# A feed-forward's first product from seven block products in groups of 768 tokens

## The chip, the cores and the metric

The kernel runs on one core of a Trainium2 chip, which has a matmul engine (PE, with its weight loads shown apart as PEld), VectorE (DVE), ScalarE (ACT), GpSimd (POOL) and SyncE (SP); SP issues nearly all DMAs here. The metric is the device time of one execution in microseconds, the median of several runs. Before the change it was 1222.69 us (three runs, 1220.99 to 1223.44).

## The reference

Three layers follow one another. An attention between 512 tokens and 32 state rows, in 8 batches and 8 heads, gives 4608 rows of 512 numbers. A mixture of 8 experts sends each row with a positive score to one expert. The last layer, which is changed here, is a feed-forward over all 4608 rows:

```python
def _moe2_ref(x, w_in, w_out):        # x 4608 x 512, w_in 512 x 2048, w_out 2048 x 512
    h = x @ w_in
    relu6 = np.clip(h + 3.0, 0.0, 6.0)
    g = h * relu6 / 6.0
    return (g @ w_out).astype(np.float32)
```

## The kernel before

Everything is float32. In this layer PE multiplies in the type `float32r`, so each operand is split: `hi` is the value cast to `float32r` (by ACT), `lo` the remainder (by DVE or POOL), and a product is the sum of three matmuls, hi by hi, hi by lo and lo by hi (`PAIRS`). 4608 tokens are 36 chunks of 128; `w_in` and `w_out` are cut into 16 blocks f of 128 hidden columns (`NFF`).

The feed-forward takes the chunks in groups of four (512 tokens), and one group of two. For a group j and a block f, `stage_a` (L1269) multiplies w_in's block by the group's transposed tokens: 12 matmuls of 512 columns (256 in the small group), three for each quarter of the 512 inputs, all into one PSUM bank. Then the gate: Relu with a bias on ACT, minimum and multiplication on DVE, the cast on ACT, the remainder on DVE. Two steps later `stage_b` (L1289) multiplies the gate by w_out's block, three matmuls of 512 columns for each chunk, adding up over all f in a PSUM bank of its own per chunk. Only after the last f is the sum scaled by 1/6 and written out. The tokens are transposed on PE and split (`turn`, L1245).

The split weights of all 16 blocks lie in SBUF for the whole stage (`W1` for w_in, `W2` for w_out). The inputs of weights are first turned from 64-bit numbers into float32 by four DVE steps a block (`Weights.cut`). That happens beside the earlier layers; blocks 0 to 2 are split right there and kept in SBUF (`steps`, L1176), blocks 3 to 15 are stored to DRAM as float32 (`keep`, L1182, tensor `w32`) and read again in the feed-forward (`again`, L1187), where `convert` splits them while the first group runs.

There is no scheduler: engines run their instructions in the order in which the code names them (`manual_schedule`), and wait on semaphores where a tile is not ready or its buffer is not free. A tile pool with `bufs=3` gives a tag three buffers; a fourth tile of that tag waits until all that used the first, DMAs among them, is done. SP too works in order: a DMA whose data is not ready keeps all later ones of SP from being issued. The tensors of the first two layers, the loops over experts (`item_a`, `item_b`) and their DMAs stay as they are.

Of the kernel before, what the change touches and what calls it, by code (L numbers as in the profile page):

```python
# [9 lines left out]
F32 = mybir.dt.float32  # L10
# [10 lines left out]
P = 128  # L21
# [656 lines left out]
class Experts:  # L678
# [108 lines left out]
    def run(self, ctx, c2, tail, plan, after):  # L787
# [272 lines left out]
        scatter_a()  # L1060
        turned32(xb[:, 0:DM], x32)
# [34 lines left out]
NPRE = 3  # L1096
# [9 lines left out]
class Weights:  # L1106


    def __init__(self, tc, ctx, w_in, w_out):
        self.tc, self.w_in, self.w_out = tc, w_in, w_out  # L1110
        self.rp = ctx.enter_context(tc.tile_pool(name="w_r", bufs=2))
        self.W1, self.W2, self.raw = {}, {}, {}
        self.w32 = tc.nc.dram_tensor("w32", (NFF, 2, P, DM), F32, kind="Internal").ap()
        self.alloc(ctx.enter_context(tc.tile_pool(name="w_c", bufs=1)), range(NPRE))

    def alloc(self, pool, fs):
        for f in fs:
            self.W1[f] = [pool.tile([P, 4, P], F32R, name=f"W1_{i}_{f}") for i in range(2)]
            self.W2[f] = [pool.tile([P, DM], F32R, name=f"W2_{i}_{f}") for i in range(2)]
# [61 lines left out]

# [5 lines left out]
    def again(self, f):  # L1187

        t = self.raw[f] = [self.room(i) for i in range(2)]
        for i in range(2):  # L1190
            self.tc.nc.sync.dma_start(t[i], self.w32[f, i])  # L1191


def ffn(tc, ctx, W, x_in, out, k):

# [48 lines left out]

    def turn(c0):  # L1245

        j, c = divmod(c0, 4) if c0 < 32 else (B, c0 - 32)
        if c == 0:
            new_xt(j)
        if j in (0, B):  # L1250

            pt = p_o.tile([P, 4, P], F32, tag=f"o{c + j // 2}", name="ptx")
        else:
            pt = p_h.tile([P, 4, P], F32, tag="h", name="ptx")
        for kk in range(4):
            nc.tensor.transpose(pt[:, kk, :], xw[c0][:, P * kk:P * kk + P], ident)  # L1256
        hi, lo = ([a[:, :, P * c:P * c + P] for a in t] for t in (xt[j] if j == 1 else [[a] for a in whole[j]]))
        parts = pt.rearrange("p (i k) t -> i p k t", i=len(hi))
        for i, h in enumerate(hi):
            nc.scalar.copy(h, parts[i])  # L1260

        def low():
            for i, h in enumerate(hi):
                nc.vector.tensor_tensor(lo[i], parts[i], h.bitcast(F32), op=ALU.subtract)  # L1264
        return low
# [3 lines left out]
    def stage_a(j, f):  # L1269
        n = P * len(cols(j))  # L1270
        ph = p_h.tile([P, 512], F32, tag="h", name="ph")
        i = 0
        for kk in range(4):
            for a, b in PAIRS:
                nc.tensor.matmul(  # L1275
                    ph[:, :n], lhsT=W1[f][a][:, kk, :], rhs=xt[j][b][kk // 2][:, kk % 2, :n],
                    start=(i == 0), stop=(i == 11),
                )
                i += 1
        gg = sp.tile([P, 512], F32, tag="gg", name="gg", bufs=1)  # L1280
        nc.scalar.activation(gg[:, :n], ph[:, :n], AF.Relu, bias=k["three"])  # L1281
        nc.vector.scalar_tensor_tensor(gg[:, :n], gg[:, :n], 6.0, ph[:, :n], op0=ALU.min, op1=ALU.mult)  # L1282
        hi, lo = g[j, f] = [sp.tile([P, 512], F32R, tag=f"g{i}", name=f"g{i}", bufs=3) for i in range(2)]
        nc.scalar.copy(hi[:, :n], gg[:, :n])  # L1284
        nc.vector.tensor_tensor(lo[:, :n], gg[:, :n], hi[:, :n].bitcast(F32), op=ALU.subtract)  # L1285

    po, o = {}, {}

    def stage_b(j, f):  # L1289
        gg = g.pop((j, f))  # L1290
        for c, c0 in enumerate(cols(j)):
            if f == 0:
                po[c0] = p_o.tile([P, DM], F32, tag=f"o{c + (4 if j == B else 0)}", name=f"po{c}")
            for i, (a, b) in enumerate(PAIRS):
                nc.tensor.matmul(  # L1295
                    po[c0], lhsT=gg[a][:, P * c:P * c + P], rhs=W2[f][b],
                    start=(f == 0 and i == 0), stop=(f == NFF - 1 and i == 2),
                )
            if f == NFF - 1:
                if j in (0, B):  # L1300
                    oc = W.room(c % 2)
                else:
                    if c % 2 == 0:
                        o[c // 2] = W.scratch(c // 2).bitcast(F32).rearrange("p (c f) -> p c f", c=2)
                    oc = o[c // 2][:, c % 2, :]
                if c % 2:
                    nc.scalar.mul(oc, po[c0], 1.0 / 6.0)  # L1307
                else:
                    nc.vector.tensor_scalar(oc, po[c0], 1.0 / 6.0, None, op0=ALU.mult)
                if 0 < j < B - 1 or (j == B - 1 and c < 2):  # L1310
                    if c % 2:
                        for p, rows in rows_of(out, c0 - 1):
                            nc.sync.dma_start(rows, o[c // 2][p])
                else:
                    for p, rows in rows_of(out, c0 - c % 2):
                        nc.sync.dma_start(rows[:, c % 2], oc[p])

    later = [0, 2, 32] + list(range(4, 32, 2))

    def fetch_after(c0):  # L1320

        n = later.index(c0 - 1) + 2 if c0 % 2 else len(later)
        if n < len(later):
            fetch(later[n])

    conv = []
    for f in range(NPRE, NFF):
        conv += [(f, lambda f=f, i=i: W.split(f, i, W.raw[f][i], nc.vector)) for i in range(2)]
        if f + 2 < NFF:
            conv.append((f, lambda f=f: W.again(f + 2)))  # L1330

    def convert(n, until=-1):

        while conv and (n > 0 or conv[0][0] <= until):
            conv.pop(0)[1]()
            n -= 1

    W.again(NPRE)
    W.again(NPRE + 1)
    fetch(0)  # L1340
    fetch(2)
    low = None
    for c in range(4):
        if low:
            low()
        low = turn(c)
        fetch_after(c)
    low()


    work = [(0, 0), (0, 1)]
    for f in range(2, NFF + 2):
        work += [(0, f)] * (f < NFF) + [(B, f - 2)]
    both = len(work)
    work += [(j, f) for j in range(1, B) for f in range(NFF)]

    turns = {1: [32, 33]}
    for c in range(4):
        turns[both - 5 + c] = [4 + c]
        for j in range(2, B):  # L1360
            turns[both + (j - 2) * NFF + 3 * c + 2] = [4 * j + c]
    last = both - 6
    total = len(conv)
    LAG = 2
    for n in range(len(work) + LAG):
        if n < len(work):
            f = work[n][1]
            if n < both:
                convert(len(conv) - total * max(0, last - n) // last, f + 1)
            stage_a(*work[n])  # L1370
        if n >= LAG:
            stage_b(*work[n - LAG])
        for low in [turn(c0) for c0 in turns.get(n, ())]:
            low()
        for c0 in turns.get(n, ()):
            fetch_after(c0)
# [132 lines left out]
```

## Time and profile before

| what | value |
|---|---|
| median of three runs | 1222.69 us |
| the profiled execution, its own time | 1233.33 us |
| its span, first to last instruction | 1231.6 us |
| mean granted PE clock | 0.984 of full |
| PE busy over the span | 1176.7 us (96%), 5916 matmuls |
| DVE, ACT, POOL busy | 537.9, 439.0, 118.8 us |
| feed-forward, first transpose to last matmul | 466.1 to 1226.6 us |
| moved by DMA over the span | 132.05 MB |

The profile is one execution taken by the hardware profiler. It took 10.6 us more than the median of the runs, so times inside it are read as they stand, and a difference between two kernels is compared with the runs. Matmuls are pipelined: a single row's duration is longer than the distance between two of them, and the distance is what counts.

### The profile page before, as it was taken

How to read it: one execution, taken by the hardware profiler on the slowest of the kernel's cores; microseconds unless marked ns; L12 is line 12 of the kernel's file. 1: busy time of each engine (PE TensorE's matmuls, PEld its weight loads, DVE VectorE, ACT ScalarE, POOL GpSimd, SP SyncE). 2: the span in 40 equal slices, each digit the busy share in tenths (PEclk: the TensorE clock that was granted, in tenths of full speed). 3: DMA queues.
4: the chain of work that ended last, by engine and by line, in shares of the span. 5: the costliest groups of instructions: out<-in, count | busy, mean ns of one | idle time of the engine just before them, and what ended most of it. 6: DMA issues, size and time to landing. Idle time of an engine off the chain costs nothing.

```text
span 1231.6 us, 16493 instructions
## 1 busy us (share of the span) xinstructions
PE 1176.7 (96%) x5916; PEld 945.1 (77%) x5916; DVE 537.9 (44%) x984; ACT 439.0 (36%) x802; POOL 118.8 (10%) x162
## 2 busy tenths in 40 slices
PE   7988898999998968999999999999999999999998
PEld 4565767887886647888888888888888888888886
DVE  6968596876873004443422322322232322322222
ACT  7865353443543103333422222322222222322222
POOL 4556131011011000000000000000000000000000
PEclk9989899999999988999999999999999999999999
DMA  7956667587585784220200000000000000000000
GB/s 194 312 193 213 213 229 248 173 280 253 169 283 180 264 289 131 69 61 27 76 27 18 35 18 18 35 18 18 35 18 18 35 18 18 35 1 1 35 1 34
DMA packets 83535, 132.05 MB, mean 107 GB/s; under 512 B 12176, under 2 KB 49040, under 8 KB 82704
## 3 DMA queue, kind: packets, MB, share of 16 engines
q1 hardware_dynamic: 78832, 119.63, 29.8%
q0 software_dynamic: 4640, 11.57, 2.6%
q8 instruction: 40, 0.66, 0.2%
q14 instruction: 23, 0.19, 0.0%
HBM read 91.55 MB, written 43.30 MB: 109 GB/s over the span
## 4 chain that ended last, share of the span: by engine, by line
PE 62%; DMA 0%; SPq 0%; DVE 0%; ACT 0%; issue 0%
PE ph L1275 30%; PE po L1295 30%; PE ptx L1256 1%; DMA xw<-x_in_dram 0%; SPq L1191 0%; DVE xt L1264 0%; ACT raw L1307 0%; ACT xt L1260 0%; SPq L1229 0%
## 5 line engine op out<-in xcount | busy, mean ns | idle before, releaser
L1295 PE MATMUL po<-W,g 128*128 128x512 f32 x1632 | 393.5, 389 | 0.0
L1295 PEld LDWEIGHTS po<-W,g 128*128 128x128 f32 x1632 | 305.3, 188 | 62.7
L1275 PE MATMUL ph<-xt,W 128*128 128x512 f32 (+1 forms) x1536 | 351.5, 378 | 1.0 <-ACT xt L1260 0.7
L1275 PEld LDWEIGHTS ph<-xt,W 128*128 128x128 f32 x1536 | 275.5, 188 | 54.0 <-ACT xt L1260 0.9
L1282 DVE SCALAR_TENSOR_TENSOR gg<-gg,ph 128x512 f32<-128x512 f32 (+1 forms) x144 | 94.9, 659 | 388.6 <-ACT gg L1281 388.6
L1281 ACT ACTIVATE gg<-ph,three 128x512 f32<-128x512 f32 (+1 forms) x144 | 95.9, 666 | 394.7 <-PE ph L1275 394.6
L1285 DVE TENSOR_TENSOR g<-gg,g 128x512 fp32r<-128x512 f32 (+1 forms) x144 | 95.5, 663 | 97.5 <-ACT g L1284 95.1
L860 PE MATMUL ph<-xTa,w1p 128*128 128x512 f32 x480 | 121.0, 403 | 4.5 <-DVE w1p L775 1.8
L1284 ACT CAST g<-gg 128x512 fp32r<-128x512 f32 (+1 forms) x144 | 86.1, 598 | 104.6 <-DVE gg L1282 104.6
L872 PE MATMUL po<-w2p,hT 128*128 128x512 f32 x480 | 120.9, 398 | 0.4 <-ACT hT L864 0.3
L860 PEld LDWEIGHTS ph<-xTa,w1p 128*128 128x128 f32 x480 | 92.3, 193 | 27.3 <-DVE w1p L775 2.5
L872 PEld LDWEIGHTS po<-w2p,hT 128*128 128x128 f32 x480 | 89.0, 188 | 21.4 <-DVE hT L865 0.8
L1275 PE MATMUL ph<-raw,W 128*128 128x512 f32 x192 | 46.6, 391 | 0.0
L277 PE MATMUL pxr<-BD,AT 128*128 128x265 f32 x128 | 41.3, 442 | 3.8 <-ACT XR L281 1.9
L1275 PEld LDWEIGHTS ph<-raw,W 128*128 128x128 f32 x192 | 35.7, 188 | 7.3
L775 DVE TENSOR_TENSOR w1p<-raw,w1p 128x512 fp32r<-128x512 f32 x48 | 32.0, 685 | 20.3 <-ACT w1p L774 10.2
L1160 ACT ACTIVATE raw<-raw 128x512 f32<-128x512 f32 x32 | 22.0, 686 | 47.9 <-DVE cv L1156 47.8
L864 ACT ACTIVATE hT<-ph 128x512 fp32r<-128x512 f32 x40 | 23.9, 596 | 42.5 <-PE ph L860 38.9
L1264 DVE TENSOR_TENSOR xt<-ptx,xt 128x512 fp32r<-128x512 f32 x30 | 20.6, 691 | 38.7 <-ACT xt L1260 38.6
L378 POOL DMA_INDIRECT xs_dram<-XR,slot x32 | 32.9, 1028 | 39.8 <-issue 20.2
L774 ACT CAST w1p<-raw 128x512 fp32r<-128x512 f32 x48 | 28.5, 618 | 20.3 <-DMA raw<-in_moe_w_dram 20.3
L865 DVE SCALAR_TENSOR_TENSOR hT<-ph,hT 128x512 fp32r<-128x512 f32 x40 | 27.5, 687 | 18.7 <-ACT hT L864 16.0
(218 smaller groups left out, 932.9 us busy)
## 6 DMA issues: line engine op xcount, KB each, us to landing
raw<-in_moe_w_dram SPq DMA_DIRECT2D x80, 512.0 KB, 6.3
raw<-in_moe_w_in_dram SPq DMA_DIRECT2D x16, 512.0 KB
raw<-in_moe_w_out_dram SPq DMA_DIRECT2D x16, 512.0 KB, 8.2
x_in_dram<-XR SPq DMA_DIRECT2D x8, 1024.0 KB
xw<-x_in_dram SPq DMA_DIRECT2D x14, 512.0 KB
w<-cv SPq DMA_DIRECT2D x26, 256.0 KB, 3.1
cv<-w SPq DMA_DIRECT2D x26, 256.0 KB
out_dram<-raw SPq DMA_DIRECT2D x13, 512.0 KB
```

What stands on the lines that cost most here:

```text
L277: nc.tensor.matmul(px, lhsT=AT[b, q][:, P * c:P * c + P], rhs=BD[:, 2 * b + q, :], start=True, stop=True,)
L378: i = nc.gpsimd.indirect_dma_start(out=xs, out_offset=bass.IndirectOffsetOnAxis(ap=slot[:, col:col + 1], axis=0), in_=t["rows"][c], in_off ...
L774: nc.scalar.copy(hi, src)
L775: (eng or nc.vector).tensor_tensor(lo, src, hi.bitcast(F32), op=ALU.subtract)
L860: nc.tensor.matmul(ph, lhsT=w1p[a][:, f, kk, :], rhs=xTa[b][:, kk, :], start=(n == 0), stop=(n == 11))
L872: nc.tensor.matmul(po[c], lhsT=hp[f][a][:, P * c:P * c + P], rhs=w2p[b][:, f, :], start=(f == 0 and n == 0), stop=(f == NF - 1 and n == 2),)
L1275: nc.tensor.matmul(ph[:, :n], lhsT=W1[f][a][:, kk, :], rhs=xt[j][b][kk // 2][:, kk % 2, :n], start=(i == 0), stop=(i == 11),)
L1281: nc.scalar.activation(gg[:, :n], ph[:, :n], AF.Relu, bias=k["three"])
L1282: nc.vector.scalar_tensor_tensor(gg[:, :n], gg[:, :n], 6.0, ph[:, :n], op0=ALU.min, op1=ALU.mult)
L1284: nc.scalar.copy(hi[:, :n], gg[:, :n])
L1285: nc.vector.tensor_tensor(lo[:, :n], gg[:, :n], hi[:, :n].bitcast(F32), op=ALU.subtract)
L1295: nc.tensor.matmul(po[c0], lhsT=gg[a][:, P * c:P * c + P], rhs=W2[f][b], start=(f == 0 and i == 0), stop=(f == NFF - 1 and i == 2),)
```

## The change

The first product is computed for pairs of blocks of f, p = 0 to 7, and for groups of six chunks (768 tokens). The weights of a pair and the tokens of a group are each taken as 2 x 2 blocks: w_in by halves of the 512 inputs and by the pair's two f, the tokens by halves of the inputs and into two halves of 384 tokens. Seven products of such blocks (in place of eight), with sums and differences of blocks as operands, give all four blocks of the result after seven additions on DVE (`strassen`). Each product is 6 matmuls of 384 columns. The second product of a pair follows one pair later: 36 matmuls of 512 columns, in six PSUM groups that are added to a sum in SBUF by DVE (by ACT for p = 0).

The combinations of the weights are made once. The first four chunks (the two of state rows and the first two) go through all 16 f in the old way. During this first round the weights come from `w32`, are split, combined (`combine`) and stored to two DRAM tensors, `wc` and `wo`; the split weights no longer stay in SBUF but have three buffers per matrix. Afterwards 40 pairs (five groups of eight) load 1.84 MB of `wc` and 1.05 MB of `wo` each. The tokens' combinations are made in `turn`. Blocks 0 to 2 are now kept in `w32` as the others are, and the first two are read again before the loop of the small experts.

```diff
         scatter_a()
+        for f in range(2):
+            for i in range(2):
+                self.W.again(f, i)
         turned32(xb[:, 0:DM], x32)
...
+    groups = [list(range(c, c + 6)) for c in range(2, 32, 6)]
...
+    def new_w(i, f):
+        (W1, W2)[i][f] = t = sp.tile([P, 2, DM], F32R, tag=f"W{i}", name=f"W{i}", bufs=3)
+        return t
+
+    def split_w(i, f):
+        t = new_w(i, f)
+        split(t[:, 0], t[:, 1], W.raw[f, i])
+
+    def combine(p):
...
+        v.tensor_tensor(s[0], a2[0], a2[1], op=ALU.add)
+        v.tensor_tensor(s[2], a1[0], a2[0], op=ALU.subtract)
+        v.tensor_tensor(s[1], s[0], a1[0], op=ALU.subtract)
+        v.tensor_tensor(s[3], a1[1], s[1], op=ALU.subtract)
+        both = qp.tile([P, 2, 2 * DM], F32R, tag="both", name="both", bufs=2)
+        split(both[:, 0], both[:, 1], t)
+        nc.sync.dma_start(W.wc[p, :, 3 * DM:].rearrange("p (i f) -> p i f", i=2), both.bitcast(F32))
+
+    def store_w(f):
+        p, o = divmod(f, 2)
+        if o == 0:
+            nc.sync.dma_start(W.wc[p, :, 0:2 * DM], W1[f].bitcast(F32).rearrange("p i f -> p (i f)"))
         else:
+            nc.sync.dma_start(
+                W.wc[p, :, 2 * DM:3 * DM].rearrange("p (i f) -> p i f", i=2), W1[f][:, :, 2 * P:].bitcast(F32)
+            )
...
+    for f in range(NFF + LAG):
+        if f < NFF:
+            stage_a(f)
+            if f + 2 < NFF:
+                load_w(0, f + 4)
+                split_w(0, f + 2)
+                if f % 2:
+                    combine((f + 2) // 2)
+            if f + 1 < NFF:
+                split_w(1, f + 1)
+                load_w(1, f + 3)
+        if f >= LAG:
+            stage_b(f - LAG)
+        if f < NFF:
+            store_w(f)
+            store_o(f)
...
+        if f >= NFF - 2:
+            load_c(f - NFF + 2) if f < NFF else load_o(f - NFF)
...
+        p1 = product(m, A11, B11)
+        nc.scalar.copy(c1, p1)
+        plus(u2, product(m, S2, T2), c1)
+        plus(u5, product(m, S1, T1), u2)
+        p7 = product(m, S3, T3)
+        plus(c22, p7, u5)
+        plus(u2, p7, u2)
+        plus(c1, product(m, A12, B21), c1)
+        done(1, 1, c22)
+        plus(u5, product(m, S4, B22), u5)
+        done(0, 0, c1)
+        plus(u2, product(m, A22, T4), u2)
+        return [lambda: done(0, 1, u5), lambda: done(1, 0, u2)]
...
+        between = []
+        if m < total:
+            between = strassen(m)
+            load_c(m + 2)
+        if m > 0:
+            second(m - 1, between)
+            load_o(m + 1)
...
         def kept(f):
-            a, steps = W.cut(W.raw.pop(f))
-            return steps + [lambda: W.keep(f, a)]
+            def begin():
+                a, steps = W.cut(W.raw.pop(f))
+                todo.extend(steps + [lambda: W.keep(f, a)])
+
+            return [begin] + [lambda: todo.pop(0)() for _ in range(9)]
```

`load_w(i, f)` reads block f of matrix i from `w32`; `store_o` stores w_out's split block; `done` is the gate for one of the four blocks.

How the change moves the instructions of ACT in the first group of tokens, before (`W_0_5` is w_in's or w_out's hi part of block 5, `cv` the block as float32, `DMAHW` a semaphore of a DMA):

```order
L1281 ACTIVATE gg<-ph,three 128x512 [waits DVE_49,PE_49]
L1284 CAST g_3271<-gg 128x512 [waits DVE_49]
L1173 CAST W_0_5_3018<-cv_3175 128x512 [waits DMAHW0_49]
L1173 CAST W_0_5_3020<-cv_3176 128x512 [waits DMAHW1_49]
L1281 ACTIVATE gg<-ph,three 128x256 [waits DVE_49,PE_49]
L1284 CAST g_3307<-gg 128x256 [waits DVE_49]
```

The same place after (`W_3311` and `W_3364` are w_in's blocks 7 and 8, `wf` w_in's block as float32, `W_3323` and `W_3367` w_out's blocks 6 and 7, `both` the combinations):

```order
L1239 CAST W_3311<-wf 128x512 [waits DMAHW1_49,DMAHW0_49]
L1239 CAST both<-raw_3314 128x1024 [waits DVE_49]
L1239 CAST W_3323<-cv_3229 128x512 [waits DMAHW5_49,DMAHW3_49,PE_49]
L1250 ACTIVATE gg<-b_3342,three 128x512 [waits PE_49,Activation_49]
L1239 CAST g_3358<-gg 128x512 [waits DVE_49]
L1239 CAST W_3364<-wf 128x512 [waits DMAHW6_49,DMAHW5_49]
L1239 CAST W_3367<-cv_3273 128x512 [waits DMAHW7_49,DMAHW1_49,PE_49]
L1250 ACTIVATE gg<-b_3386,three 128x512 [waits DVE_49,PE_49]
```

A cast of a weight block waited for one DMA, its load, and now waits for two: its load, and the store of the block whose buffer it takes (for block 8 that of block 5).

SP in the same stretch, before: loads of the weights, one after the other as buffers come free.

```order
L1191 DMA cv_3385<-w 128x512 [waits DMAHW6_49,DMAHW2_49,DVE_49]
L1191 DMA cv_3386<-w 128x512 [waits DMAHW7_49,DMAHW3_49,DVE_49]
L1191 DMA cv_3451<-w 128x512 [waits DMAHW4_49,DVE_49]
L1191 DMA cv_3452<-w 128x512 [waits DMAHW5_49,DVE_49]
L1191 DMA cv_3517<-w 128x512 [waits DMAHW6_49,DVE_49]
```

After, over two values of f (`W_3267` and `W_3311` are w_in's blocks 6 and 7):

```order
L1178 DMA cv_3370<-w 128x512 [waits DMAHW0_49,DVE_49]
L1284 DMA wc<-W_3267 128x1024 [waits DMAHW1_49]
L1292 DMA wo<-W_3323 128x1024 [waits DMAHW2_49]
L1178 DMA wf<-w 128x512 [waits DMAHW3_49]
L1279 DMA wc<-both 128x2048 [waits DMAHW4_49,DVE_49]
L1178 DMA cv_3423<-w 128x512 [waits DMAHW5_49,DVE_49]
L1286 DMA wc<-W_3311 128x2x256 [waits DMAHW6_49]
L1292 DMA wo<-W_3367 128x1024 [waits DMAHW7_49]
```

Five stores now stand between the loads; the store of block 7 comes behind the combinations' store and a load.

DVE in the middle of the stage, before: two operations for a block f and a group.

```order
L1282 SCALAR_TENSOR_TENSOR gg<-gg,ph 128x512 [waits Activation_49]
L1285 TENSOR_TENSOR g_5687<-gg,g_5686 128x512 [waits PE_49,Activation_49]
L1282 SCALAR_TENSOR_TENSOR gg<-gg,ph 128x512 [waits Activation_49]
L1285 TENSOR_TENSOR g_5719<-gg,g_5718 128x512 [waits PE_49,Activation_49]
L1264 TENSOR_TENSOR xt_5422<-ptx,xt_5421 128x4x128 [waits Activation_49]
```

After, the first 12 of 21 operations of a pair (`b` are PSUM banks of products, `o` of the second product, `c` and `cv` sums in SBUF):

```order
L1411 TENSOR_TENSOR c_5645<-b_5660,c_5644 128x384 [waits PE_49,Activation_49]
L1411 TENSOR_TENSOR cv_5646<-b_5668,c_5645 128x384 [waits DVE_49,PE_49]
L1411 TENSOR_TENSOR cv_5647<-b_5676,cv_5646 128x384 [waits DVE_49,PE_49]
L1411 TENSOR_TENSOR c_5645<-b_5676,c_5645 128x384
L1411 TENSOR_TENSOR c_5644<-b_5685,c_5644 128x384 [waits PE_49]
L1251 SCALAR_TENSOR_TENSOR cv_5693<-cv_5693,cv_5647 128x384 [waits Activation_49]
L1240 TENSOR_TENSOR g_5651<-cv_5693,g_5650 128x384 [waits Activation_49]
L1411 TENSOR_TENSOR cv_5646<-b_5698,cv_5646 128x384 [waits PE_49]
L1251 SCALAR_TENSOR_TENSOR cv_5706<-cv_5706,c_5644 128x384 [waits Activation_49]
L1240 TENSOR_TENSOR g_5649<-cv_5706,g_5648 128x384 [waits Activation_49]
L1411 TENSOR_TENSOR c_5645<-b_5711,c_5645 128x384 [waits PE_49]
L1458 SCALAR_TENSOR_TENSOR W_5259<-o_5721,W_5259 128x512 [waits PE_49]
```

Additions and gates stand in turn in DVE's one order, and the sums of the second product behind them.

## Rows read from the trace of the kernel before

**Rows 1.** The page: its head, and the chain that ended last
```profile
span 1231.6 us, 16493 instructions
...
PE 62%; DMA 0%; SPq 0%; DVE 0%; ACT 0%; issue 0%
PE ph L1275 30%; PE po L1295 30%; PE ptx L1256 1%; DMA xw<-x_in_dram 0%; SPq L1191 0%; DVE xt L1264 0%; ACT raw L1307 0%; ACT xt L1260 0%; SPq L1229 0%
```

**Rows 2.** Busy time by stage: stretch, length, busy per engine, clock, DMA share, GB/s
```profile
466.00:1227.00 761.00, 759.50 (x3496) 632.33 (x3496) 240.53 (x369) 224.45 (x369) 0.00 (x0) 1.00 0.09 29
```

**Rows 3.** Program in order of time, PE alone: start, length, engine, line, tiles, count
```profile
466.09 3.27 PE L1256 MATMUL ptx<-ident,xw 128*128 128x128 f32 x16 [13.81 <-DMA xw<-x_in_dram]
...
482.57 1.60 PE L1275 MATMUL ph<-xt,W 128*128 128x256 f32 x12
484.00 2.91 PE L1295 MATMUL po<-W,g 128*128 128x512 f32 x12
...
800.36 2.88 PE L1275 MATMUL ph<-xt,W 128*128 128x512 f32 x12
803.08 2.88 PE L1295 MATMUL po<-W,g 128*128 128x512 f32 x12
...
811.25 0.60 PE L1256 MATMUL ptx<-ident,xw 128*128 128x128 f32 x4
811.60 0.71 PE L1275 MATMUL ph<-xt,W 128*128 128x512 f32 x2
...
1218.30 8.32 PE L1295 MATMUL po<-W,g 128*128 128x512 f32 x36
```

**Rows 4.** Stretches of stores (1227) and of loads (459.5); landings of 256 KB stores
```profile
1227.00:1227.50 0.50, 0.00 (x0) 0.00 (x0) 0.00 (x0) 0.25 (x1) 0.00 (x0) 1.00 1.01 401
1227.50:1228.00 0.50, 0.00 (x0) 0.00 (x0) 0.00 (x0) 0.00 (x0) 0.00 (x0) 1.00 1.00 410
459.50:462.50 3.00, 0.00 (x0) 0.00 (x0) 0.00 (x0) 0.00 (x0) 0.00 (x0) 0.50 0.95 299
...
DMA to landing us min/median/max: 2.0/3.1/5.1
```

**Rows 5.** The chain in order of time where the feed-forward begins: SP's issues
```profile
458.59 0.36 SPq L1191
...
459.00 0.42 SPq L1191
```

**Rows 6.** Groups by line and shape, 480 to 1232 us: busy, mean ns | idle before
```profile
L1285 DVE TENSOR_TENSOR g<-gg,g 128x512 fp32r<-128x512 f32 x126 | 87.3, 693 | 86.6 <-ACT g L1284 86.6
L1284 ACT CAST g<-gg 128x512 fp32r<-128x512 f32 x126 | 78.4, 622 | 95.1 <-DVE gg L1282 95.1
L1285 DVE TENSOR_TENSOR g<-gg,g 128x256 fp32r<-128x256 f32 x16 | 6.8, 425 | 9.5 <-ACT g L1284 7.1 <-issue 2.4
L1284 ACT CAST g<-gg 128x256 fp32r<-128x256 f32 x16 | 6.5, 407 | 7.8 <-DVE gg L1282 7.8
```

**Rows 7.** DVE in order of time, three operations behind one another
```profile
146.91 0.68 DVE L775 TENSOR_TENSOR w1p<-raw,w1p 128x512 fp32r<-128x512 f32 x1
147.51 0.69 DVE L775 TENSOR_TENSOR w2p<-raw,w2p 128x512 fp32r<-128x512 f32 x1
148.11 0.68 DVE L865 SCALAR_TENSOR_TENSOR hT<-ph,hT 128x512 fp32r<-128x512 f32 x1
```

**Rows 8.** Busy time where the loop of the small experts begins
```profile
385.00:390.00 5.00, 3.32 (x10) 2.61 (x11) 0.00 (x0) 0.58 (x1) 3.00 (x6) 0.69 0.21 76
```

**Rows 9.** One line's instructions: the split of the first weight blocks, min/median/max ns
```profile
L1174 POOL TENSOR_TENSOR W<-cv,W x6: 1297/1316/1457, 58.7 to 173.1; 128x512 fp32r<-128x512 f32 x6
L1173 ACT CAST W<-cv x6: 605/620/672, 55.7 to 172.0; 128x512 fp32r<-128x512 f32 x6
```

**Rows 10.** Busy time around a gap of PE
```profile
170.00:175.00 5.00, 2.82 (x11) 1.61 (x9) 4.83 (x5) 3.33 (x6) 2.78 (x2) 1.00 1.03 373
175.00:180.00 5.00, 4.24 (x13) 3.40 (x14) 4.83 (x9) 1.22 (x2) 0.00 (x0) 0.66 0.99 349
```

More of the change, by code (lines that the diff above doesn't have):

```diff
@@ new lines, in split, with new_g, gate, halves @@
+    def split(hi, lo, src, copy=nc.scalar.copy):
+        copy(hi, src)
+        nc.vector.tensor_tensor(lo, src, hi.bitcast(F32), op=ALU.subtract)
+    g = {}
+    def new_g(key):
+        g[key] = [sp.tile([P, 2 * HALF], F32R, tag=f"g{i}", name=f"g{i}", bufs=4) for i in range(2)]
+        return g[key]
+    def gate(h, gg):
+        nc.scalar.activation(gg, h, AF.Relu, bias=k["three"])
+        nc.vector.scalar_tensor_tensor(gg, gg, 6.0, h, op0=ALU.min, op1=ALU.mult)
+    def halves(t):
+        return [t[:, i] for i in range(2)]
@@ new lines, in ffn, with stage_b, out_first @@
+    pos = []
+    def stage_b(f):
+        gg = g.pop(("f", f))
+        for c in range(4):
+            if f == 0:
+                pos.append(out_bank())
+            for n, (a, b) in enumerate(PAIRS):
+                nc.tensor.matmul(
+                    pos[c], lhsT=gg[a][:, P * c:P * c + P], rhs=W2[f][:, b], start=(f == 0 and n == 0),
+                    stop=(f == NFF - 1 and n == 2),
+                )
+    def out_first():
+        for u in range(2):
+            c0 = first[2 * u][0]
+            oc = new_w(u, "out").bitcast(F32)
+            nc.scalar.mul(oc[:, 0], pos[2 * u], 1.0 / 6.0)
+            nc.vector.tensor_scalar(oc[:, 1], pos[2 * u + 1], 1.0 / 6.0, None, op0=ALU.mult)
+            for p, rows in rows_of(out, c0):
+                nc.sync.dma_start(rows, oc[p])
@@ L1278, in stage_a, with product @@
+    A11, A12, A22, S1, S2, S3, S4 = range(7)
+    B11, B21, B22, T1, T2, T3, T4 = range(7)
+    bank_of = [0]
+    def product(m, a, b):
+        w, (o, d), t = wc[m], AT7[a], bank(bank_of[0] % 4)[:, 0:HALF]
+        bank_of[0] += 1
+        i = 0
+        for kk in range(2):
+            for u, x in PAIRS:
+                s = o + d * u + P * kk
+                nc.tensor.matmul(
+                    t, lhsT=w[:, s:s + P], rhs=XC[m // NP][:, x, b, kk, :], start=(i == 0), stop=(i == 5)
                 )
@@ L1287, in ffn @@
[L1287 to L1336, printed above, removed]
@@ L1362, in ffn @@
[L1362 to L1373, printed above, removed]
-            low()
-        for c0 in turns.get(n, ()):
-            fetch_after(c0)
+        return t
@@ new lines, in ffn, with second @@
+    acc = {}
+    def second(m, between):
+        n, p = divmod(m, NP)
+        gs = [g.pop((m, i)) for i in range(2)]
+        w = wo.pop(m)
+        for c in range(6):
+            i, h = divmod(c, 2)
+            if p == 0 and h == 0:
+                acc[i] = new_w(n % 2, ("out", n, i)).bitcast(F32)
+            po = out_bank()
+            o = HALF * h + P * i
+            q = 0
+            for f in range(2):
+                for a, b in PAIRS:
+                    nc.tensor.matmul(
+                        po, lhsT=gs[f][a][:, o:o + P], rhs=w[:, DM * (2 * f + b):DM * (2 * f + b) + DM],
+                        start=(q == 0), stop=(q == 5),
+                    )
+                    q += 1
+            dst = acc[i][:, h]
+            if p == 0:
+                nc.scalar.mul(dst, po, 1.0 / 6.0)
+            else:
+                nc.vector.scalar_tensor_tensor(dst, po, 1.0 / 6.0, dst, op0=ALU.mult, op1=ALU.add)
+            if c < 2 and between:
+                between.pop(0)()
+            if p == NP - 1:
+                c0 = groups[n][2 * i]
+                if n == len(groups) - 1 and i == 2:
+                    for q, rows in rows_of(out, c0):
+                        nc.sync.dma_start(rows[:, h], acc[i][q, h])
+                elif h == 1:
+                    for q, rows in rows_of(out, c0):
+                        nc.sync.dma_start(rows, acc[i][q])
@@ new lines, in ffn, with fetch_next @@
+    pairs = [c for cs in groups for c in cs[::2]]
+    def fetch_next():
+        if pairs:
+            fetch(pairs.pop(0))
+    fetch(32, True)
+    fetch(0, True)
+    for f in range(2):
+        split_w(0, f)
+    load_w(0, 2)
+    load_w(0, 3)
+    split_w(1, 0)
+    combine(0)
+    todo = []
+    for c, (c0, h) in enumerate(first):
+        pt = transposed(out_bank(), xw[c0][:, h])
+        split(xt[0][:, :, P * c:P * c + P], xt[1][:, :, P * c:P * c + P], pt)
+    load_w(1, 2)
+    fetch_next()
@@ new lines, in ffn @@
+    out_first()
+    q0.close()
+    cp1 = ctx.enter_context(tc.tile_pool(name="f_c1", bufs=1))
+    turns = {1: 0, 3: 1, 5: 2}
+    total = NP * len(groups)
+    for m in range(total + 1):
+        n, p = divmod(m, NP)
+        between = []
[5 more added lines that the diff above has]
+            load_o(m + 1)
+        for left in between:
+            left()
+        for low in todo:
+            low()
+        todo = []
+        if m < total and p in turns and n + 1 < len(groups):
+            if p == 1:
+                new_xc(n + 1, cp1 if n % 2 == 0 else cp)
+            todo.append(turn(n + 1, turns[p], [out_bank(), out_bank()]))
+            fetch_next()
```

208 lines of the change are left out of this document (112 added, 96 removed).

## The prediction

> **What bounds the kernel now.** Read the chain of waits first, then the busy times by stage, then the program in order of time. The chain gives 62% of the span to PE, 60% to the feed-forward's two matmul lines [rows 1]. By stage PE has no gap there: 759.5 us busy of the 761 from 466 to 1227, with the clock at full speed, DVE at 240.5 us and ACT at 224.5 us, DMA at 9% [rows 2]. So every microsecond of PE work removed comes off the end, and whatever makes PE wait is added to it; nothing else in this stage has been near a limit.
>
> **PE's work.** Twelve 512-column matmuls stand 803.08 - 800.36 = 2.72 us apart, 0.2267 each; twelve of 256 take 484.00 - 482.57 = 1.43, 0.119 each; four transposes 0.35 [rows 3]. The two widths differ by 0.42 ns a column, so 384 columns should take 0.173 us. No row shows that width: it could not be under 0.119 nor over 0.2267, and since both known widths lie on one line with the weight load hidden I take the line.
> Before: 3168 x 0.2267 + 192 x 0.119 + 34 x 0.35 = 753 us, and the stage takes 466.09 to 1226.6, 760.5: 7.5 us of start (cold clock, first waits) beside it. After: a first round of 512 tokens done the old way, 384 x 0.2267 = 87.1; then 40 pairs (five groups of 768 tokens, eight pairs of f) of seven products x 6 matmuls x 0.173 = 7.27 and 36 x 0.2267 = 8.16, together 15.43 each, 617.2; and 34 x 0.35 = 11.9. Sum 716. PE has 37 us less to do.
>
> **The first round.** Here the gain is lost. Over 16 values of f the round also splits all the weights, writes the split parts and combinations to DRAM, and every weight tile has three buffers. The order of ACT shows it: the cast that fills the first matrix's tile of f+2 waits for two DMAs, its load and the store of the tile of f-1, which had the same buffer. Before, the same cast waits for a load alone. So a loop runs over two values of f, through SP's one queue and the in-order ACT and DVE, without PE in it:
> A. From the issue of the 1.05 MB combination store to the landing of the odd f's 0.26 MB store queued behind it and a 0.26 MB load. Writes of this kind ran at 401 and 410 GB/s, loads of 2 KB rows at 299 [rows 4]; the 0.26 MB store has pieces of 1 KB, for which I take 299 too: 2.6 + 0.9 + 0.9 = 4.4. A 0.26 MB store took 2.0 us to land at best, 3.1 in the middle, 5.1 at worst, so 1.3 beyond its 0.66 of transfer at best [rows 4]; an issue takes SP 0.36 to 0.42 [rows 5]. Together 6.1.
> B. Landing to the next store's issue: the cast 0.62, its remainder on DVE 0.69, the second matrix's remainder 0.60 behind it (pipelined DVE instructions start 0.60 apart), since SP's next load needs that buffer [rows 6, 7]: 1.9.
> C. Even f: two issues 0.84, load 0.9, store of 0.52 MB 1.3, landing 1.3: 4.3.
> D. Landing to the combination store: cast 0.62, remainder 0.69, four 256-wide operations at 0.42 (0.40 started behind one another) 1.6, then a cast and a remainder of 1024 elements. Those two widths are not in the rows; by the slopes of rows 6 (0.84 and 1.05 ns an element) 1.05 and 1.23. With hops 5.3.
> Sum 17.6 us for two f, where PE needs 48 x 0.2267 = 10.9. Casts for f = 3 to 15 wait, 13, or 6.5 turns of the loop: 6.5 x 6.7 = 44 us. Ends of the loop: if the 1.3 already holds SP's own 0.4, and all transfers run at 401, 16.1 a turn (+34); with landings of 3.1 - 0.66 = 2.4 and all at 299, 21 (+66). I take 17.6, near the quiet landing, because this loop has few transfers in flight. Behind the waiting cast stand, on ACT, the next matrix's cast, the Relu and the cast of the gate; behind them DVE's half of the gate; PE's next product waits for that very cast.
> At the round's end some 3.4 MB of stores and fetches stand before the first 1.84 MB load of the second round: 5.2 MB at 349 to 400 from the last combination store [rows 4, 10] is 14 to 16 us, while PE has about 11 left. With the last two steps, which have no product to run beside the gate, 8 us.
>
> **The second round.** DVE has 15 operations of 384 and 6 of 512 in a pair's 15.43 us. Pipelined (0.60 for 512, so 0.46) that is 10.5; each at its own duration (0.69; 0.56 between 0.425 and 0.69) 12.5; the four gates stop DVE for ACT's cast, 4 x 0.6 = 2.4 [rows 6, 7]. So 12.9 to 14.9: under PE, closely. Turning a group's tokens adds 5 x 0.42 + 0.69 + 1.23 = 4.0 to three of eight pairs of four groups, 12 in all; by the lower figure 1.5 us each passes PE and later pairs take most back: 4 us. By the upper one 12 x 3.5 = 42. ACT has 9 casts and Relus of 384 (some 5 us). DMA needs 2.9 MB a pair, 187 GB/s against the 299 to 410 seen, each load issued a pair ahead: nothing.
>
> **The rest.** Four weight loads, formerly ahead of the token fetch (459 to 463 us), now stand before the small experts' loop, where DMA is at 0.21 [rows 8]: they cost nothing, and the fetch gains four issues of 0.42, 1.7, less what its ten own issues take: 1.5 at most. Three weight blocks earlier no longer need six ACT casts of 0.62 and six POOL subtractions of 1.32 [rows 9] but six stores; PE is full there or waits for others: 0, from -2 to +2. A second cold start, after the wait for the first product, 1.7; hidden elsewhere (below).
>
> **Sum.** -37 + 44 + 8 + 4 + 1.7 - 1.5 = +19. The profiled execution took 1233.33 us (span 1231.6, 1.7 around it), 10.6 above the median of the runs, 1222.69; the sum is a difference and is put on the median: 1242.
>
> **The clock.** After a stretch in which PE was busy 2.82 of 5 us the next five show 0.66 of full speed, 68% of it at 1.2 GHz, worth 1.7 us of PE's work [rows 10]. The loop leaves PE idle some 6 us once a turn, so 10.9 becomes 12.6, still inside 17.6: nothing. The Trainium skill, TensorE: Matmul & The Clock Gate, section HAM oscillation, says that a wait between bursts of matmuls sends the clock back every time, and that the kernel pays at each; the rows agree that it falls. What differs is that the price would stand only where PE is what the others wait for: then 6.5 x 1.7 = 11 us more, 1253.
>
> **Rivals.**
> 1. The stores get out of the way (faster). If the landings did not hold the casts, the first round would run at PE's pace: 1242 - 44 = 1198. The transfers alone would allow it: loads of 7.3 MB at 299, stores of 23 at 401 and 3.4 of other fetches at 349 [rows 10] are 92 us against PE's 91. For it: DMA had 9% of this stage, and 2.0 us to land is less than PE's work per f. Against: two landings, two waits in SP's order and a 5 us chain on ACT and DVE follow one another in each turn. It decides below 14.7 us a turn, where 6.5 x (14.7 - 10.9) = 25 equals the rest.
> The Trainium skill, DMA: Bandwidth & Descriptors, section Where 436 GB/s comes from, puts about 358 GB/s on transfers between HBM and SBUF. By that the 3.93 MB of two f take 11.0 us, as long as PE, and this rival would give 1199; the 401 and 410 GB/s of [rows 4] are above it, and the rows are followed.
> 2. DVE becomes the bound of the second round: its order and the casts inside each gate cost the upper 42: 1280. For: 12.9 to 14.9 of 15.4 leaves little. Against: the sums to be added wait for PE anyway, so the pipelined figure is the nearer.
> 3. The slow clock is paid: 1253, from above.
> 4. The change does not do what it says: 384 columns cost as much as 512 (0.2267). Then the products gain nothing: 1680 x 0.054 = 90 us more, 1332. Against: 256 columns stand at 0.119.
>
> **How the numbers follow.** Forecast 0.68, its own range 1229 to 1262 (turns of 16.1 to 20, second round 0 to 8). Rival 1: 0.14; rival 2: 0.10; rival 3: 0.06; rival 4: 0.02. A range of 1222 to 1264 leaves out most of rival 1, half of rival 2 and rival 4, some 0.2. About 0.2% (2.4 us) is what a measurement of this kernel can tell from no change. Faster by more: rival 1 and a tail of the forecast's lower end, 0.15; within: 0.06; slower: 0.79.
>
> **What would show it.** Right: PE below 70% busy for some 140 us after the stage's start, with a gap of 5 to 7 us every 17 to 18, ended by ACT's cast of the first weight tile, that in turn by a DMA; then 40 stretches of 15.4 to 16.6 us with PE full, DVE near 75 to 85%, 384-column matmuls 0.173 apart. Wrong: a first round of about 100 us (rival 1), PE waiting for DVE inside the second round's pairs (rival 2), or a second-round pair that is not 15.4 us long when PE is full.

## The result, and the profile after

| | median us | runs | ratio to before, 95% interval |
|---|---|---|---|
| before | 1222.82 | 4, from 1220.99 to 1223.44 | |
| after | 1239.78 | 4, from 1234.73 to 1242.53 | 1.0137, 1.0097 to 1.0176 |

The change makes the kernel 17 us slower; 1242 was forecast. The profiled execution of after lasted 1242.09 us (span 1240.3, mean clock 0.973).

The page of after, its busy times and the chain that ended last (before: [rows 1]):

```profile
PE 1160.9 (94%) x6060; PEld 970.1 (78%) x6060; DVE 845.5 (68%) x1640; ACT 503.0 (41%) x955; POOL 110.9 (9%) x156
...
PE 51%; DMA 6%; DVE 3%; ACT 2%; issue 1%; SPq 1%; ACTq 0%; DVEq 0%
PE o L1449 26%; PE b L1397 23%; DMA wc<-W 4%; DVE W L1240 1%; PE o L1235 1%; DMA wc<-wc 1%; ACT W L1239 1%; ACT both L1239 1%; PE b L1308 0%; DMA wo<-W 0%; DMA raw<-x_in_dram 0%; SPq L1178 0%; ACT g L1239 0%; SPq L1217 0%; DVE raw L1276 0%
```

PE's share of the chain fell from 62% to 51%, and a store that had no place in it, from a split weight tile W to wc in DRAM, has 4%. The busy times by stage say where (columns: stretch, length, busy time and instructions of PE, PEld, DVE, ACT and POOL, granted clock, DMA share, GB/s); the first row is the first round, the second nearly all of the second round, to be held against [rows 2]:

```profile
453.80:599.80 146.00, 111.17 (x425) 85.13 (x425) 73.77 (x124) 53.81 (x87) 0.00 (x0) 0.89 0.67 240
...
632.00:1230.00 598.00, 598.00 (x3034) 539.30 (x3034) 454.90 (x851) 221.20 (x410) 0.00 (x0) 1.00 0.54 195
```

The second round has no gap on PE, and DVE is at 76%: PE bounds it. The first round has 35 us of gaps and a clock of 0.89. Who waited for whom in it (total us, times, longest):

```profile
ACT W L1239 <- DMA wc<-W: 40.5, 13, 5.7
PE b L1308 <- ACT W L1239: 25.4, 7, 6.7
```

Thirteen waits of the cast for a store, as counted ahead. One turn of the loop on SP's queue and on ACT, in order of time (start, length, engine, line, tiles, and in brackets the wait ahead):

```profile
496.76 0.32 SPq L1279 DMA_DIRECT2D wc<-both  x1
...
497.75 1.20 SPq L1286 DMA_DIRECT2D wc<-W  x1
...
504.59 0.33 SPq L1178 DMA_DIRECT2D cv<-w  x1
504.96 0.43 SPq L1284 DMA_DIRECT2D wc<-W  x1
...
514.04 0.32 SPq L1279 DMA_DIRECT2D wc<-both  x1
...
531.27 0.32 SPq L1279 DMA_DIRECT2D wc<-both  x1
```

```profile
502.62 0.62 ACT L1239 CAST W<-wf 128x512 fp32r<-128x512 f32 x1 [4.03 <-DMA wc<-W]
...
508.87 0.62 ACT L1239 CAST W<-wf 128x512 fp32r<-128x512 f32 x1 [3.06 <-DMA wc<-W]
```

The four parts read off these rows: A, combination store issued at 496.76 to the cast at 502.62, 5.9 us; B, to SP's next load at 504.59, 2.0; C, to the next cast at 508.87, 4.3; D, to the next combination store at 514.04, 5.2. Together 17.3 (the next turn 17.2). PE in the same stretch and across into the second round:

```profile
503.29 4.87 PE L1308 MATMUL b<-xt,W 128*128 128x512 f32 x12 [3.93 <-ACT W L1239]
508.00 2.93 PE L1325 MATMUL o<-W,g 128*128 128x512 f32 x12
510.76 2.88 PE L1308 MATMUL b<-xt,W 128*128 128x512 f32 x12
513.49 2.88 PE L1325 MATMUL o<-W,g 128*128 128x512 f32 x12
520.61 4.87 PE L1308 MATMUL b<-xt,W 128*128 128x512 f32 x12 [4.24 <-ACT W L1239]
...
587.19 3.31 PE L1325 MATMUL o<-W,g 128*128 128x512 f32 x12 [1.86 <-ACT g L1239]
591.50 3.29 PE L1325 MATMUL o<-W,g 128*128 128x512 f32 x12 [1.00 <-ACT g L1239]
599.76 13.24 PE L1397 MATMUL b<-xc,wc 128*128 128x384 f32 x66 [4.96 <-DMA wc<-wc]
614.60 3.41 PE L1397 MATMUL b<-xc,wc 128*128 128x384 f32 x18 [1.59 <-ACT c L1421]
...
690.14 1.25 PE L1235 MATMUL o<-ident,raw 128*128 128x128 f32 x8
691.14 7.53 PE L1397 MATMUL b<-xc,wc 128*128 128x384 f32 x42
698.51 8.36 PE L1449 MATMUL o<-wo,g 128*128 128x512 f32 x36
706.71 7.47 PE L1397 MATMUL b<-xc,wc 128*128 128x384 f32 x42
714.02 8.36 PE L1449 MATMUL o<-wo,g 128*128 128x512 f32 x36
...
1219.62 16.52 PE L1449 MATMUL o<-wo,g 128*128 128x512 f32 x72
```

From start to start, 42 matmuls of 384 columns take 714.02 - 706.71 = 7.31 us, 0.174 each, and 36 of 512 take 8.20, 0.228 each: a pair 15.51 (15.43 forecast), and one in which `turn` also transposes tokens (8 transposes), 690.14 to 706.71, 16.57. The feed-forward, from its first transposes at 453.80 to 1236.14, takes 782.3 us against 760.5 before.

### The profile page after: what moved, and what is told of

Same layout as the page of the kernel before. It is cut to its first block, busy times and chain, and to the rows that moved or that the text cites. A ratio compares the mean times of both kernels' runs of the same rounds, so it can differ in the third digit from the quotient of the medians.

```text
span 1240.3 us, 17749 instructions
## 1 busy us (share of the span) xinstructions
PE 1160.9 (94%) x6060; PEld 970.1 (78%) x6060; DVE 845.5 (68%) x1640; ACT 503.0 (41%) x955; POOL 110.9 (9%) x156
## 4 chain that ended last, share of the span: by engine, by line
PE 51%; DMA 6%; DVE 3%; ACT 2%; issue 1%; SPq 1%; ACTq 0%; DVEq 0%
PE o L1449 26%; PE b L1397 23%; DMA wc<-W 4%; DVE W L1240 1%; PE o L1235 1%; DMA wc<-wc 1%; ACT W L1239 1%; ACT both L1239 1%; PE b L1308 0%; DMA wo<-W 0%; DMA raw<-x_in_dram 0%; SPq L1178 0%; ACT g L1239 0%; SPq L1217 0%; DVE raw L1276 0%
## 5 line engine op out<-in xcount | busy, mean ns | idle before, releaser
L1449 PE MATMUL o<-wo,g 128*128 128x512 f32 x1440 | 334.3, 390 | 0.0
L1449 PEld LDWEIGHTS o<-wo,g 128*128 128x128 f32 x1440 | 269.7, 188 | 54.7
L1397 PE MATMUL b<-xc,wc 128*128 128x384 f32 x1680 | 301.2, 337 | 6.6 <-DMA wc<-wc 5.0
L1397 PEld LDWEIGHTS b<-xc,wc 128*128 128x128 f32 x1680 | 293.7, 189 | 9.3 <-issue 5.4
L1240 DVE TENSOR_TENSOR g<-cv,g 128x384 fp32r<-128x384 f32 x160 | 89.3, 558 | 92.8 <-ACT g L1239 92.8
L1239 ACT CAST g<-cv 128x384 fp32r<-128x384 f32 x160 | 82.2, 514 | 157.0 <-DVE cv L1251 157.0
L1458 DVE SCALAR_TENSOR_TENSOR W<-o,W 128x512 f32<-128x512 f32 x210 | 134.6, 681 | 3.5 <-PE o L1449 3.3
L1250 ACT ACTIVATE cv<-cv,three 128x384 f32<-128x384 f32 x80 | 49.3, 616 | 143.8 <-DVE cv L1411 136.3
L1411 DVE TENSOR_TENSOR c<-b,c 128x384 f32<-128x384 f32 x160 | 87.0, 551 | 23.8 <-PE b L1397 23.2
L1308 PE MATMUL b<-xt,W 128*128 128x512 f32 x192 | 60.7, 472 | 26.1 <-ACT W L1239 25.4
```

Source lines behind the costliest of these rows:

```text
L1240: nc.vector.tensor_tensor(lo, src, hi.bitcast(F32), op=ALU.subtract)
L1250: nc.scalar.activation(gg, h, AF.Relu, bias=k["three"])
L1308: nc.tensor.matmul(ph, lhsT=W1[f][:, a, P * kk:P * kk + P], rhs=xt[b][:, kk, :], start=(n == 0), stop=(n == 11))
L1397: nc.tensor.matmul(t, lhsT=w[:, s:s + P], rhs=XC[m // NP][:, x, b, kk, :], start=(i == 0), stop=(i == 5))
L1411: v.tensor_tensor(c, t, u, op=ALU.add)
L1449: nc.tensor.matmul(po, lhsT=gs[f][a][:, o:o + P], rhs=w[:, DM * (2 * f + b):DM * (2 * f + b) + DM], start=(q == 0), stop=(q == 5),)
```

## The experiments

"FFN" below is that stretch, from the first transposes to the end of the last product, each from its own profile. The first four kernels ran on one chip, the other three on another, each beside runs of the kernel before.

| kernel | median us | before, same chip | ratio, 95% interval | first transposes at | FFN us |
|---|---|---|---|---|---|
| before again | 1223.75 (one run) | 1222.24 | | 456.4 | 760.6 |
| early stores | 1195.92 | 1222.24 | 0.9786, 0.9767 to 0.9804 | 446.3 | 744.3 |
| five buffers | 1198.68 | 1222.24 | 0.9802, 0.9779 to 0.9826 | 450.3 | 743.2 |
| early stores and fetches | 1192.51 | 1222.24 | 0.9741, 0.9716 to 0.9765 | 449.0 | 737.9 |
| changed again | 1246.85 | 1231.44 | 1.0130, 1.0105 to 1.0155 | 455.2 | 783.9 |
| split put back | 1248.41 | 1231.44 | 1.0137, 1.0119 to 1.0155 | 462.3 | 782.8 |
| combination last | 1240.83 | 1231.44 | 1.0085, 1.0061 to 1.0108 | 450.2 | 782.3 |

**Before again.** No edit.

> The kernel before, unchanged, profiled once more. The shown profile of before lasted 10.6 us longer than the median of its runs, and the profile of the changed kernel reaches the feed-forward's first transposes at 453.8 us where that of before reaches them at 466.1: 12.3 us earlier, while the change should win 1.5 us there at most. Theory A: most of the 12 us is this one execution of before, in the layers ahead of the feed-forward; then this profile reaches the first transposes at 454 to 459 us and lasts about 1223 us. Theory B: the change really wins 12 us ahead of the feed-forward; then the first transposes stand at 465 to 467 us again. The feed-forward itself should take 760 to 761 us in both.

The first transposes stand at 456.4: most of the 12 us was that one execution of before. What the change itself does there shows behind the last products of the small experts. PE in before again, and then in after, from those products on:

```profile
439.76 2.74 PE L1045 MATMUL pob<-raw,xn 128*128 128x512 f32 x6
456.41 3.53 PE L1256 MATMUL ptx<-ident,xw 128*128 128x128 f32 x16 [13.91 <-DMA xw<-x_in_dram]
460.61 0.49 PE L1275 MATMUL ph<-xt,W 128*128 128x512 f32 x1 [0.68 <-ACT xt L1260]
```

```profile
439.83 3.17 PE L1045 MATMUL pob<-raw,xn 128*128 128x512 f32 x7
453.80 1.94 PE L1235 MATMUL o<-ident,raw 128*128 128x128 f32 x8 [10.81 <-DMA raw<-x_in_dram]
456.60 1.97 PE L1235 MATMUL o<-ident,raw 128*128 128x128 f32 x8 [0.86 <-DMA raw<-x_in_dram]
459.29 11.08 PE L1308 MATMUL b<-xt,W 128*128 128x512 f32 x36 [0.72 <-issue]
```

The first transposes come 3.1 us sooner after those products (this wait is 13.8 and 13.9 us in the two profiles of before, and 10.7 to 11.3 in all seven of kernels with the change), but the second half of the tokens is waited for again; to the first matmul of the feed-forward's products it is 18.1 us before and 16.3 after.

**Early stores.** The same stores from the same buffers, issued earlier:

```
                 split_w(0, f + 2)
+                store_w(f + 2)
                 if f % 2:
                     combine((f + 2) // 2)
...
                 split_w(1, f + 1)
+                store_o(f + 1)
...
-        if f < NFF:
-            store_w(f)
-            store_o(f)
```

(and `store_w(0)`, `store_w(1)` and `store_o(0)` ahead of the loop.)

> The changed kernel, with one thing moved: each store of a split weight tile is issued right behind that tile's split, two steps (first matrix) or one step (second matrix) before PE uses the tile, so ahead of the combination store and not behind it. Same bytes, same buffers, same arithmetic. Theory A (the turn hangs on the landing of the store of the tile of f-1, queued behind the combination store): the store has landed long before the buffer is wanted again; a turn falls from 17.3 us to PE's 10.9 to 11.5, 6.5 turns win 38 to 42 us, and the kernel takes about 1199 us (1194 to 1206), faster than before. Rival B (the queue's transfers are the limit: 3.9 MB a turn): a turn stays near 17 us, 1235 to 1242. Rival C (the ACT and DVE chain of split and combination is the limit, and the store only seems to end the wait): a turn of 14 to 16 us, 1215 to 1230.

1195.92: theory A. The middle of the first round, busy times, and PE at the start of a product, two values of f apart:

```profile
465.00:540.00 75.00, 74.42 (x339) 61.20 (x337) 55.90 (x98) 41.16 (x68) 0.00 (x0) 1.00 0.92 337
```

```profile
465.46 2.88 PE L1308 MATMUL b<-xt,W 128*128 128x512 f32 x12
...
476.34 2.88 PE L1308 MATMUL b<-xt,W 128*128 128x512 f32 x12
```

PE is full at full clock with the same bytes, two values of f take it 10.88 us, and a store no longer stands among the things that ACT waited for. Rivals B and C are out, since the transfers and the chain on ACT and DVE are the same as in after. FFN falls by 38.0 us. Rival B was not far: DMA is now at 0.92, so the transfers have little room left beside PE's work.

**Five buffers.** The stores where the change put them:

```
     def new_w(i, f):
-        (W1, W2)[i][f] = t = sp.tile([P, 2, DM], F32R, tag=f"W{i}", name=f"W{i}", bufs=3)
+        if i == 0 and f in (3, 4, 8, 9, 13):
+            t = sp.tile([P, 4 * DM], F32R, tag="wo", name="wo")[:, 0:2 * DM].rearrange("p (i f) -> p i f", i=2)
+        else:
+            t = sp.tile([P, 2, DM], F32R, tag=f"W{i}", name=f"W{i}", bufs=3)
+        (W1, W2)[i][f] = t
```

> The changed kernel with its stores where they were, but five buffers in place of three for the first matrix's split tiles during the first round (f = 3, 4, 8, 9 and 13 lie in buffers that are idle until the second round). Theory A (the wait is for the buffer, because its store has not landed): the cast of f+2 then needs the store of f-3, which is two steps older; a turn falls to 10.9 to 11.5 us until f = 13, and the kernel takes about 1201 us (1195 to 1208). Rival B (transfers are the limit) and rival D (it is the loads, queued behind the stores in SP's order, that come late, and not the buffer): no change, 1235 to 1242, with the cast then waiting for its load.

1198.68, FFN 39.1 us less: theory A again, by the other end of the same wait. The loads behind the stores (rival D) are not what came late. Its first round:

```profile
469.00:545.00 76.00, 73.35 (x333) 59.88 (x331) 56.88 (x102) 40.54 (x69) 0.00 (x0) 1.00 0.93 337
```

**Early stores and fetches.** On top of the early stores:

```
+    LOADS = {12: lambda: load_c(0), 13: lambda: load_o(0), 14: lambda: load_c(1), 15: lambda: load_o(1)}
...
-        if f >= NFF - 2:
-            load_c(f - NFF + 2) if f < NFF else load_o(f - NFF)
+        if f in LOADS:
+            LOADS[f]()
```

> As the kernel with the early stores, and the first four fetches of the second round (two of the first matrix's combined weights, two of the second's) are issued at f = 12 to 15 of the first round and not at its end. The first product of the changed kernel waited 5.0 us for its fetch. Theory A (the round's end costs what I put at 8 us in the sum, of which the fetch behind the stores is the larger part): 3 to 6 us less than with the early stores alone, about 1195 us. Rival B (the fetches only push the last stores and loads back, and the last two steps wait for the gate anyway): no difference, within 2 us.

FFN falls by 6.4 us and the median by 3.4: theory A. PE where the second round begins, with early stores alone and then with both:

```profile
546.13 3.30 PE L1325 MATMUL o<-W,g 128*128 128x512 f32 x12 [1.03 <-ACT g L1239]
553.49 13.93 PE L1397 MATMUL b<-xc,wc 128*128 128x384 f32 x66 [4.06 <-DMA wc<-wc]
```

```profile
548.99 3.29 PE L1325 MATMUL o<-W,g 128*128 128x512 f32 x12 [0.98 <-ACT g L1239]
552.12 7.47 PE L1397 MATMUL b<-xc,wc 128*128 128x384 f32 x42
560.39 4.41 PE L1397 MATMUL b<-xc,wc 128*128 128x384 f32 x24 [0.81 <-DMA wc<-wc]
```

The wait of 4.06 us for the first fetch is gone, 0.81 is left at the second. The slow clock behind that wait is gone with it: 66 products took 13.93 us, of which 2.4 are more than 66 x 0.174, and the first 42 now take 7.47. All three kernels with the wait taken away beat before and after; this one is the fastest, 30 us below before.

**Changed again.** No edit; the control of the last two.

> The changed kernel, unchanged, beside the next two on one chip: 1235 to 1243 us, ratio 1.010 to 1.018, FFN from its first transposes to the last product 782 us (780 to 784).

The time is above the range, because this chip ran the kernel before at 1231.44 too; the ratio and the FFN came as expected.

**Split put back.** Ahead of the feed-forward:

```
-                todo.extend(steps + [lambda: W.keep(f, a)])
+                also = [lambda i=i: halved(f, i, a[i]) for i in range(2)] if f < 3 else []
+                todo.extend(steps + also + [lambda: W.keep(f, a)])
...
+        def halved(f, i, src):
+            t = w_c.tile([P, 2, DM], F32R, name=f"halved_{i}_{f}")
+            nc.scalar.copy(t[:, 0], src)
+            nc.gpsimd.tensor_tensor(t[:, 1], src, t[:, 0].bitcast(F32), op=ALU.subtract)
```

> The changed kernel with one removed part put back ahead of the feed-forward: the first three weight blocks are again split there (six ACT casts of 512 and six POOL subtractions, into tiles that nothing reads), beside the six stores that the change put in their place. In the profiles so far the feed-forward's first transposes stand at 466 and 456 us in the kernel before and at 446, 449, 450 and 454 us in kernels with the changed front part; 1.5 us of that is the fetch. Theory A (the removed casts and subtractions were in the way there; my nought for this part was too small): 3 to 8 us slower than the changed kernel, 1242 to 1248. Theory B (they were hidden, as I put it; the rest is spread between executions): within 2 us of the changed kernel. The feed-forward itself stays at 782 us by both.

The median is 1.6 us above the changed kernel, inside theory B's 2, but the runs of the two overlap (1244.8 to 1249.2 and 1248.4 to 1251.0). Four runs of each do not tell 1.6 from nothing, nor from the 3 us where theory A began; FFN is unchanged, as by both.

**Combination last.**

```
+        held.append((p, both))
...
             store_w(f)
+            if held:
+                store_both()
             store_o(f)
```

> The changed kernel with one store moved: the store of the combinations (1.05 MB) is issued behind the odd step's store of the first matrix's tile and not ahead of it; all else in its place. By the loop, part A loses that transfer and one issue, 2.6 + 0.4 = 3.0 us, but the even step's 0.52 MB store and loads now stand behind it, so part C can get up to 2.6 back. Theory A (a loop through the queue, whose parts follow one another): a turn of 14.3 to 16.9 us, of which 16.4 is my value, since most is given back; 6.5 turns win 3 to 20 us, about 1233 (1220 to 1237). Rival (the landing is what matters, not what stands in the queue ahead of it): a turn stays at 17.3 and the time at 1240.

SP's queue in this kernel (L1292 and L1290 are the stores of the odd and the even tile, L1285 the combination's):

```profile
509.27 0.33 SPq L1178 DMA_DIRECT2D cv<-w  x1
509.65 0.43 SPq L1292 DMA_DIRECT2D wc<-W  x1
510.13 0.47 SPq L1285 DMA_DIRECT2D wc<-both  x1
...
514.79 0.33 SPq L1178 DMA_DIRECT2D cv<-w  x1
515.17 0.76 SPq L1290 DMA_DIRECT2D wc<-W  x1
...
527.13 0.33 SPq L1178 DMA_DIRECT2D cv<-w  x1
527.51 0.43 SPq L1292 DMA_DIRECT2D wc<-W  x1
```

A and B together, from the turn's first store to SP's next load, are 514.79 - 509.65 = 5.1 us where they were 504.59 - 496.76 = 7.8. Of the 2.7 that are gone (3.0 were priced), 1.0 are the two issues ahead of the odd tile's store (497.75 - 496.76); counted from that store's own issue it is 5.1 against 6.8, so standing behind the 1.05 MB transfer cost 1.7 and not 2.6. C and D are 527.51 - 514.79 = 12.7 where they were 9.45. So all of the gain is given back: five turns in a row, from odd store to odd store, take 17.0, 17.1, 17.9, 16.3 and 19.4, in the mean 17.5; the same five in after make 17.6, and FFN is 782.3, as in after.

The forecast (16.4 a turn, 1220 to 1237 us) was missed, and turn and median are the rival's. Only the parts speak against the rival: what stands ahead of the store does count, and what is put behind it comes back in the next part. The loop does not explain either why the median lies 6 us below the control: 1.6 us of it is in FFN, the rest lies ahead of the feed-forward, where the two kernels have the same code. Its cause stays open.

## Why the prediction was right

**PE's work, -37.** 384 columns stand 0.174 apart (0.173 taken from the line between two widths), so rival 4 is out. Forty pairs at 15.51 are 620.4, not 617.2: the gain is 34, 3 us short. The counts are right for 34 chunks, 4352 rows (8 batches of 512 tokens and 32 state rows); the 4608 rows and 36 chunks named ahead of the prediction are wrong.

**The first round, +44.** The mechanism, its place and its count held: thirteen casts, each waiting for the store of the tile that had its buffer. A, B, C and D measured 5.9, 2.0, 4.3 and 5.2 against 6.1, 1.9, 4.3 and 5.3. Both kernels that take the wait away, one by the order of stores and one by buffers, win 38 to 39 us, so my 44 was some 5 too large: 2 from the turn (17.3, not 17.6), and 2.4 because in three turns PE also transposes tokens (0.8 us each), inside the loop's waits, and my sum has these a second time in PE's work. Rival 1 failed on its condition, not its arithmetic: the transfers alone do fit under PE's work, as the early stores show, but the order of SP's queue, with three buffers, kept them from it.

**The round's end, +8.** The waits in after's rows are 1.86 and 1.00 us for the gate and 4.96 for the first fetch, 7.8. My way there was less exact: 5.2 MB at 349 to 400 GB/s are 13 to 15 us, not 14 to 16, and the fetch was there 16.2 us after the last combination store was issued (583.52 to 599.76). Fetching earlier wins 6.4 us of FFN, all of it where the second round opens: 4.3 of waits (4.06 and 1.59 with early stores, 0.81 and 0.54 with both) and about 2 of slow clock. The waits for the gate stay (1.63 and 1.03 us, then 1.64 and 0.98).

**The second round, +4.** Eight of the twelve pairs in which tokens are transposed take 16.57 - 15.51 = 1.06 us longer, the first of each group 0.87; 0.70 of each are the transposes. The rest is 8 x 0.36 + 4 x 0.17 = 3.6 us. That the size agrees is luck, for its form was another than I gave: not the products wait, but the transposes, for DVE to free the output bank (total us, times, longest):

```profile
PEld o L1235 <- DVE W L1458: 3.9, 16, 0.3
```

**Cold start, +1.7.** The whole of the second round, 599.76 to 1236.14, is 636.4; less 620.4 for forty pairs and 12.0 for the transposing pairs' extra it leaves 4.0. Of this 66 x (13.24 / 66 - 0.174) = 1.8 is the low clock of the first products, as forecast, and 1.59 the wait at 614.60, which my sum did not have.

**The sum.** By these rows the terms are -34, +38.5, +8, +3.6 and +4: 20, where FFN grew by 21.8 and 20.7 was forecast; 2 us of it have no row here. The number is this near in part by luck: the two largest terms were off by 3 and 5 us in opposite directions.

**The clock.** Busy times around one gap, of the product behind it and of those that follow:

```profile
503.30:508.00 4.70, 4.70 (x13) 3.42 (x13) 2.55 (x4) 1.66 (x3) 0.00 (x0) 0.64 0.61 200
508.00:516.00 8.00, 8.00 (x37) 6.57 (x35) 4.64 (x9) 3.40 (x5) 0.00 (x0) 1.00 0.45 178
```

After a gap of 3.93 us the product took 508.00 - 503.29 = 4.71 us for what takes 2.73 at full clock, at a granted 0.64, which is 72% of the time at 1.2 GHz and the rest at 2.4: 2.0 us lost. The products behind the other five gaps took 4.46 to 5.00. A turn still ended when the loop did, at 17.3, with PE waiting for the cast again, so it was not paid, and rival 3 is out. The Trainium skill, TensorE: Matmul & The Clock Gate, section HAM oscillation, has the kernel pay at each such wait; the rows agree on the fall and not on the payment.

This is also why two of my signs were off, with the mechanism right: I looked for PE below 70% and gaps of 5 to 7 us. PE was at 111.17 of 146, 76%, and behind a first gap of 6.7 us the gaps were 3.3 to 4.2, since a matmul at half clock counts as busy twice as long. Without the 12 us that the six slow products lost, PE would have been at 68%.

**Ahead of the feed-forward.** To the first transposes the fetch won 3.1 us, of which 1.3 are lost again before the first product, inside FFN: 1.8 (1.5 at most forecast). The split of three blocks was worth 1.6 by its return, inside my -2 to +2 but not clear of noise. By stage, from the profiles of before again and after, FFN grew by 21.7, the first transposes came 2.6 sooner and the end behind the last product is 0.8 shorter: +18.3, which is the difference of the two executions (1242.09 - 1223.75). The medians say +17.0, because this execution of after lay 2.3 us above its median and that of before again 0.9 above that of before.

## What to carry to other kernels

A DMA store is a reader of its SBUF tile: the tile's next writer waits until the store has landed (13 times, 40.5 us here), and a transfer issued ahead of it on the same queue adds to that (1.7 us for 1.05 MB). Issue the store as soon as its data are there, not where its tile is last used, and look for writers that now wait for two DMAs and not one; the order of the stores alone was worth 38 us here. Where a round is to write its results to DRAM for later rounds, price the loop through the queue, turn by turn, beside the sum of bytes: the bytes fitted here, the order did not.

## What the runs showed of the hardware

The early stores and fetches kept the DMA engines at 353 GB/s for 84 us beside a PE that was busy for 81.30 of them:

```profile
468.00:552.00 84.00, 81.30 (x365) 65.81 (x364) 62.36 (x108) 45.44 (x75) 0.00 (x0) 1.00 0.97 353
```

That lies between the loads at 299 and the stores at 401 [rows 4], near the 366 that rival 1's sum makes (33.7 MB in 92 us), with PE, DVE and ACT all at work. The Trainium skill, DMA: Bandwidth & Descriptors, section Where 436 GB/s comes from, has about 358 GB/s bind between HBM and SBUF; this stretch is at that figure, while the stores alone in [rows 4] were above it. So were the fetches and stores while the second round of after opens: 400 GB/s from 599.76 to 613.00, at a DMA share of 1.03. On this one core, then, it was no ceiling.

Five kernels with the same instructions ahead of the feed-forward reached it between 446 and 455 us, the kernel before reached it at 466.1 us in one execution and 456.4 in another, and it took 1222 us on one chip and 1231 on another. A difference of 5 us that no stage's rows carry should be held against such a spread first.
